# Evacuating the first PSUM transposes of a four-layer network in two pieces of two column blocks

**Chip, cores, metric.** One core of one Trainium2 chip. The metric is the device time of one execution in microseconds, here the median of several executions. The profile of a kernel is one execution; its span, from the first instruction to the last, is about 1.8 us shorter than the time of the same execution.

## The reference

Four residual layers on 2048 tokens of width 1024: linear attention, gated MLP, and the same two again, each behind a layernorm.

```python
x = A_x                                                   # 1 x 2048 x 1024, bf16
x = x + _A_ref(_layernorm(x, axis=-1), A_wqkv, A_wo)      # linear attention, 32 heads of 32
x = x + _B_ref(_layernorm(x, axis=-1), B_W_gate, B_W_up, B_W_down)   # 3584 wide, ReLU gate
x = x + _A_ref(_layernorm(x, axis=-1), A_wqkv, A_wo)
x = x + _B_ref(_layernorm(x, axis=-1), B_W_gate, B_W_up, B_W_down)
```

## The kernel before

Only the head matters here: the first 18 us, in which four row tiles of x (128 tokens each) are loaded, normalised, transposed on TensorE and multiplied with the key weights. All later transposes are made by DMA. The loads (`k0` is the first block of 512 key columns, `k1` the second, 1 MB each; ScalarE's queue where `nc.scalar` stands, else SyncE's):

```python
    for _ in range(12):                                   # warm-up of TensorE
        nc.tensor.matmul(idle, lhsT=zero[:, 0:P], rhs=zero, start=True, stop=True)
    k0, k1, v0, q0, q1 = (ring.place() for _ in range(5))
    self.load_x(0, 0)
    self.load_x(0, 1, nc.scalar)
    k0(0, H)
    self.load_x(1, None, nc.scalar)
    k0(H, 2 * H)
    self.load_x(2)
    k1()
    ...                                                   # cut: the other loads
```

Four transposes of 128x128 blocks go into one PSUM tile, and one instruction evacuates all four, that is, copies them to SBUF, where the projection matmuls read them:

```python
    def turn(j, h):
        tp = self.ps3.tile([P, H, P], BF16, tag="b")      # H = 4
        for i in range(H):
            kt = h * H + i
            nc.tensor.transpose(tp[:, i, :], xn[j][:, kt * P:(kt + 1) * P], self.ident)
        dst = self.xnT[0, 0][:, h * H:(h + 1) * H, j * P:(j + 1) * P]

        def take(engine):
            if engine == "v":
                nc.vector.tensor_copy(out=dst, in_=tp)
            else:
                nc.scalar.activation(out=dst, in_=tp, func=ACT.Copy)
        return take
```

The first unit of the head, in the order in which each engine gets its work. `k(0, 0, between)` is the projection of row tile 0 on the first key block: eight matmuls of 128x512, with `between` put in ahead of the seventh.

```python
    def block0():
        stat(0, 0); stat(0, 1); rstd(0)
        stat(1, 0)                        # statistics of row tile 1, first half
        scale(0, 0); scale(0, 1)          # normalise row tile 0 (VectorE)
        t0 = turn(0, 0)
        t1 = turn(0, 1)
        t0("s")                           # the evacuation that the change splits
        stat(1, 1); rstd(1)
        t1("v")
        k(0, 0, between)
    def between():
        scale(1, 0)
        t0 = turn(1, 0)
        scale(1, 1)
        t0("v")
```

## Time and profile before

| | before |
|---|---|
| time, median of 3 runs | 1629.09 us (1628.83 to 1629.37) |
| span of the profiled run | 1627.0 us |
| TensorE busy | 1621.9 us |
| TensorE idle for a named wait | 1.3 + 0.4 + 0.2 us, all before 7.5 us |
| first evacuation, start to first projection matmul | 6.79 to 7.44 us |

Read it from below: the kernel is a stream of matmuls with almost no gap, so a change either takes matmul time away or closes a gap; and the gaps are in the head. The lines that carry this stand in the prediction.

### The profile page before, as it was taken

To read this page: it belongs to the slowest core of one execution; us is meant where nothing else is said; L and a number is where in the kernel's file an instruction comes from. 1 tells how busy PE (TensorE), PEld (TensorE's weight loads), DVE (VectorE), ACT (ScalarE), POOL (GpSimd) and SP (SyncE) were. 2 spreads that over 40 slices of the span, in tenths; PEclk is the share of its full clock that TensorE was granted. 3 is DMA by queue.
4 is the path that set the end of the run, shared out by engine and by line. 5 is a ranking of instruction groups with operands and counts; after the bars stand their busy time and mean duration, and the time that the engine had idled before them with its cause. 6 is when DMAs were issued, how large, how long until landed. Compare 5 with 4: busy or idle time off the path is not lost.

```text
span 1627.0 us, 18776 instructions
## 1 busy us (share of the span) xinstructions
PE 1621.9 (100%) x7756; PEld 740.3 (46%) x7756; DVE 566.7 (35%) x940; ACT 331.8 (20%) x638; POOL 201.9 (12%) x134
## 2 busy tenths in 40 slices
PE   9999999999999999999999999999999999999999
PEld 4444444444444444444444444444444444444444
DVE  7845695213112212222264547932021112111211
ACT  6741212101110110111067312121011101101110
POOL 2349220000000000000023582100000000000000
PEclk9999999999999999999999999999999999999999
DMA  8313547447445445544560147464554454454452
GB/s 253 58 52 61 173 75 210 144 147 227 155 158 188 156 147 166 168 149 134 168 121 1 52 99 247 86 190 146 187 165 150 156 179 155 145 168 152 155 162 72
DMA packets 298246, 235.06 MB, mean 144 GB/s; under 512 B 101296, under 2 KB 294192, under 8 KB 298160
## 3 DMA queue, kind: packets, MB, share of 16 engines
q1 hardware_dynamic: 293120, 229.27, 48.0%
q10 hardware_dynamic: 5040, 4.59, 0.8%
q8 instruction: 60, 0.98, 0.2%
q14 instruction: 26, 0.21, 0.0%
HBM read 201.33 MB, written 8.39 MB: 129 GB/s over the span
## 4 chain that ended last, share of the span: by engine, by line
PE 98%; ACT 1%; DVE 1%; issue 0%; DMA 0%; DVEq 0%
PE pg L640 24%; PE pu L640 24%; PE acc L664 23%; PE ps L405 12%; PE ps L531 7%; PE ps L440 7%; PE kv L453 0%; PE acc_last L664 0%; ACT e L352 0%; DMA x<-in_A_x_dram 0%; ACT e L351 0%; PE fold L516 0%; DVE st L139 0%; ACT e L353 0%; DVE slab L359 0%
## 5 line engine op out<-in xcount | busy, mean ns | idle before, releaser
L640 PEld LDWEIGHTS <-t 128*128 128x128 bf16 x3584 | 350.7, 98 | 422.8
L640 PE MATMUL pg<-xnT,t 128*128 128x512 bf16 x1792 | 423.3, 379 | 0.0
L640 PE MATMUL pu<-xnT,t 128*128 128x512 bf16 x1792 | 423.3, 379 | 0.0
L664 PE MATMUL acc<-t,hT 128*128 128x512 bf16 x1764 | 382.5, 379 | 0.0
L646 DVE TENSOR_TENSOR hT<-pu,rg 128x512 bf16<-128x512 f32 x224 | 154.8, 691 | 572.1 <-PE pu L640 572.1
L645 ACT ACTIVATE rg<-pg 128x512 f32<-128x512 f32 x224 | 133.5, 596 | 737.3 <-PE pg L640 737.0
L664 PEld LDWEIGHTS <-hT 128*128 128x128 bf16 x1820 | 178.1, 98 | 209.0
L405 PE MATMUL ps<-t,xnT 128*128 128x512 bf16 x1024 | 224.1, 379 | 0.5 <-ACT xnT L268 0.4
L405 PEld LDWEIGHTS <-xnT 128*128 128x128 bf16 x1024 | 99.3, 98 | 120.2 <-issue 2.0
L531 PE MATMUL ps<-T,pqT 128*128 128x512 bf16 x512 | 111.2, 379 | 0.0
L146 ACT ACTIVATE rstd<-mv,eps 128x1 f32<-128x1 f32 x64 | 18.7, 294 | 333.8 <-DVE mv L144 333.6
L681 DVE TENSOR_TENSOR xo<-x,acc 128x512 bf16<-128x512 f32 x31 | 21.3, 688 | 170.3 <-PE acc L664 170.3
L484 POOL TENSOR_TENSOR prod<-pq,zrow 128x1024 f32<-128x1024 bf16 x32 | 68.0, 2124 | 85.9 <-DVE den L489 72.5
L139 DVE BATCH_NORM_STATS2 stats<-x 128x6 f32<-128x512 f32 (+1 forms) x120 | 78.0, 673 | 0.8
L531 PEld LDWEIGHTS <-pqT 128*128 128x128 bf16 x512 | 49.9, 98 | 60.4 <-issue 0.5
L420 POOL CAST ksum<-x 128x512 f32<-128x512 bf16 x2 | 1.7, 866 | 605.4 <-DVE x L359 605.4
L678 DVE TENSOR_TENSOR x<-x,acc 128x512 f32<-128x512 f32 x32 | 21.6, 674 | 138.5 <-PE acc L664 137.4
L422 POOL TENSOR_TENSOR ksum<-ksum,slab 128x512 f32<-128x512 f32 x46 | 54.0, 1182 | 84.6 <-DVE slab L359 75.1
L359 DVE SCALAR_TENSOR_TENSOR pq<-ps,e 128x512 bf16<-128x512 f32 x64 | 44.0, 688 | 53.9 <-ACT e L353 52.2
L496 POOL TENSOR_TENSOR pq<-pq,den 128x1024 bf16<-128x1024 bf16 x32 | 61.7, 1934 | 3.1 <-DVE den L491 3.1
L489 DVE TENSOR_REDUCE den<-prod 128x32 f32<-128x1024 f32 x32 | 38.9, 1217 | 53.9 <-POOL prod L484 53.9
L440 PE MATMUL ps<-slab,x 128*128 128x512 bf16 x256 | 56.6, 379 | 0.0
(57 smaller groups left out, 596.8 us busy)
## 6 DMA issues: line engine op xcount, KB each, us to landing
t<-in_B_W_gate_dram SPq DMA_DIRECT2D x56, 1024.0 KB, 7.0
t<-in_B_W_up_dram SPq DMA_DIRECT2D x56, 1024.0 KB, 5.4
t<-in_B_W_down_dram SPq DMA_DIRECT2D x64, 896.0 KB, 5.2
t<-in_A_wqkv_dram SPq DMA_DIRECT2D x11, 1024.0 KB, 5.1
t<-in_A_wo_dram SPq DMA_DIRECT2D x4, 1024.0 KB, 6.8
away<-x SPq DMA_DIRECT2D x8, 512.0 KB, 4.3
x<-away SPq DMA_DIRECT2D x8, 512.0 KB, 8.4
out_dram<-xo ACTq DMA_DIRECT2D x31, 128.0 KB, 2.3
```

Of the source, the lines that this page charges most:

```text
L139: self.nc.vector.bn_stats(out=stats[:, c, :], in_=src[:, c * fmax:(c + 1) * fmax])
L359: nc.vector.scalar_tensor_tensor(out=out, in0=ps, scalar=0.0, in1=e, op0=ALU.max, op1=ALU.add)
L405: nc.tensor.matmul(by_row(ps), lhsT=self.xnT[l, l_q][:, kt, j * P:(j + 1) * P], rhs=w[:, kt, :].rearrange("p (b i d) -> p i b d", i=R, d=H ...
L422: nc.gpsimd.tensor_tensor(out=ksum[:, cols], in0=ksum[:, cols], in1=pk, op=ALU.add)
L440: nc.tensor.matmul(ps, lhsT=self.xn[l, t][:, d * P:(d + 1) * P], rhs=self.pk[l, t][:, h * NW:(h + 1) * NW], start=(t == 0), stop=(t == sel ...
L484: nc.gpsimd.tensor_tensor(out=prod, in0=pq_of[sc, j], in1=zrow, op=ALU.mult)
L496: nc.gpsimd.tensor_tensor(out=heads(pq), in0=heads(pq), in1=den[:, :].unsqueeze(2).to_broadcast([P, D // HD, HD]), op=ALU.mult)
L531: nc.tensor.matmul(ps, lhsT=pqT[sc][:, g, j * P:(j + 1) * P], rhs=T[g // 2][:, g % 2, n2 * NW:(n2 + 1) * NW], start=(g == 0), stop=(g == G ...
L640: nc.tensor.matmul(ps, lhsT=w[:, kt, fi * P:(fi + 1) * P], rhs=self.xnT[l, q][:, kt, :], start=(kt == 0), stop=(kt == KT - 1))
L645: nc.scalar.activation(out=rg, in_=pg, func=ACT.Relu)
L646: nc.vector.tensor_tensor(out=h[:, fi, :], in0=pu, in1=rg, op=ALU.mult)
L664: nc.tensor.matmul(ps[:, 0:n], lhsT=hT[ft // 4][:, ft % 4, j * P:(j + 1) * P], rhs=wd[:, k, i * n:(i + 1) * n], start=(ft == 0), stop=(ft ...
```

## The change

Its intent: let the first projection matmul, which needs only the first transposed block, start when half of the evacuation is done.

```diff
             def take(engine):
                 if engine == "v":
                     nc.vector.tensor_copy(out=dst, in_=tp)
+                elif engine == "s":
+                    nc.scalar.activation(out=dst, in_=tp, func=ACT.Copy)
                 else:
-                    nc.scalar.activation(out=dst, in_=tp, func=ACT.Copy)
+                    for i in range(0, H, 2):
+                        nc.scalar.activation(out=dst[:, i:i + 2, :], in_=tp[:, i:i + 2, :],
+                                             func=ACT.Copy)
@@
-            t0("s")
+            t0("ss")
```

## The prediction

> **What bounds the kernel now.** I read the page first: busy shares, then the chain that ended last.
>
> ```profile
> PE 1621.9 (100%) x7756; PEld 740.3 (46%) x7756; DVE 566.7 (35%) x940; ACT 331.8 (20%) x638; POOL 201.9 (12%) x134
> ...
> PE 98%; ACT 1%; DVE 1%; issue 0%; DMA 0%; DVEq 0%
> ```
>
> TensorE is busy for 1621.9 of 1627.0 us and it makes 98% of the chain. So only 5.1 us of the span can be had by anything that is not fewer or faster matmuls, and ScalarE, busy 20%, is no bound in the large. The change adds and removes no matmul. It can matter only in a gap of TensorE, or where ScalarE itself is the chain. So next I asked which waits TensorE has at all, in the view of waits for that engine over the whole span (columns: us in total, times, longest):
>
> ```profile
> PE idle L221 <- DVE zero L218: 1.3, 1, 1.3
> PE ps L405 <- ACT xnT L268: 0.4, 1, 0.4
> PE tp L261 <- DVE x L155: 0.2, 1, 0.2
> ```
>
> These are three waits, all in the first 7.5 us. The middle one is the very wait that the change aims at: the first projection matmul waits for ScalarE's evacuation (L268) of the first four transposes. Then the first microseconds in order of time (start, duration, engine, line, and in brackets the idle time before):
>
> ```profile
> 5.90 0.72 DVE L155 TENSOR_SCALAR x<-x,mv,rstd 128x512 bf16<-128x512 bf16 x2
> 6.35 0.72 PE L261 MATMUL tp<-ident,x 128*128 128x128 bf16 x8 [0.21 <-DVE x L155]
> 6.79 0.60 ACT L268 ACTIVATE xnT<-tp 128x512 bf16<-128x512 bf16 x1 [1.24 <-PE tp L261]
> 7.25 0.21 DVE L144 BATCH_NORM_AGGREGATE mv<-st 128x2 f32<-128x12 f32 x1
> 7.38 0.37 DVE L266 COPY xnT<-tp 128x512 bf16<-128x512 bf16 x1
> 7.44 1.47 PE L405 MATMUL ps<-t,xnT 128*128 128x512 bf16 x6 [0.37 <-ACT xnT L268]
> 7.50 0.29 ACT L146 ACTIVATE rstd<-mv,eps 128x1 f32<-128x1 f32 x1
> 8.06 0.74 DVE L155 TENSOR_SCALAR x<-x,mv,rstd 128x512 bf16<-128x512 bf16 x2 [0.31 <-ACT rstd L147]
> 8.74 0.39 PE L261 MATMUL tp<-ident,x 128*128 128x128 bf16 x4
> 8.97 0.59 PE L405 MATMUL ps<-t,xnT 128*128 128x512 bf16 x2
> ...
> 13.31 0.60 ACT L349 ACTIVATE e<-ps 128x512 f32<-128x512 f32 x1 [0.58 <-PE ps L405]
> ...
> 13.81 1.08 ACT L268 ACTIVATE xnT<-tp 128x512 bf16<-128x512 bf16 x2
> ```
>
> The reader should see: the eight transposes end at 7.07 (6.35 + 0.72); the first evacuation starts at 6.79, as soon as its four are done, and ends at 7.39; the matmul starts 0.05 us later, at 7.44. TensorE is idle for 0.37 us in between. Then six matmuls run, at most, before four transposes of the second row tile, which need a scaling (L155) that starts at 8.06. Last, the chain of waits itself, cut to the first 10 us:
>
> ```profile
> 6.35 0.41 PE tp L261 x4
> 6.76 0.02 issue
> 6.79 0.61 ACT xnT L268
> 7.39 0.05 issue
> 7.44 1.47 PE ps L405 x6
> 8.91 0.22 PE tp L261 x4
> 9.13 0.43 PE ps L405 x2
> 9.56 0.24 PE tp L261 x4
> 9.80 0.02 issue
> 9.82 0.42 DVE xnT L266
> ```
>
> The evacuation is a link of the chain that sets the end. What is saved there is saved at the end, if nothing beside it takes over.
>
> **What the Trainium skill says.** "ScalarE: Activation LUTs", section "What ACT_TABLE_LOAD costs": an ACTIVATE with immediate scale and bias takes 186 ns + 0.833 ns per element of a partition, and back-to-back ones overlap by about 93 ns. The trace agrees roughly: 512 elements should be 612 ns, and L268 shows 597 (0.60). Two of them back to back at 13.81 take 1.08 us in place of 2 x 0.597 = 1.19, so the overlap here is 0.11. "TensorE: Matmul & The Clock Gate", section "Back-to-back issue gap": N / 2.4 + 2.5 ns for a warm matmul on its own, 216 ns for 512 columns; the six matmuls of 1.47 us with 0.379 for one give (1.47 - 0.379) / 5 = 0.218, so it agrees. "Perfetto Trace Analysis", section "DVE / Act Engine Instruction": the profile's end is when the semaphore update is pushed, and it becomes visible after that; the 0.05 us between 7.39 and 7.44 is that.
>
> **The change part by part.** The order of instructions of both builds differs in three places only: one 128x512 ACTIVATE becomes two of 128x256 on ScalarE, the ScalarE counts that later instructions wait for rise by one, and the weight load of the third projection matmul gets a wait of its own (for the second piece). TensorE, VectorE, GpSimd and the transfers have the same instructions in the same order.
>
> Removed: nothing of the start. The first piece still waits for all four transposes, since only the last of them signals. So ScalarE still starts at 6.79.
>
> First piece: 0.597 - 256 x 0.833 ns (0.213) = 0.384 us, so it ends at 6.79 + 0.384 = 7.17; the skill's formula gives 0.399. With the 0.05 the first matmul can start at 7.22 to 7.23. Are its other inputs there? Its transposes are done at 7.07 and the next four hold the TensorE no longer than that. The first half of its weights was issued at 1.19 and landed 4.5 us later, at 5.7. So the start moves from 7.44 to 7.23, a gain of 0.21.
>
> Second piece: two pieces together cost one fixed part more, less the overlap: 0.384 + 0.384 - 0.11 = 0.65 us in place of 0.60, so it ends at 6.79 + 0.65 = 7.44, visible at 7.49. The third matmul, which waits for it, would start at 7.23 + 2 x 0.217 = 7.66. There is no wait there, with 0.17 to spare.
>
> Fifth and sixth matmul: at 7.23 + 4 x 0.217 = 8.10. They need VectorE's copy (7.38 + 0.37 = 7.75) and the second half of the weights (estimate from the median of both halves, 5.2, and the first, 4.5: some 5.9 after 1.7, so 7.6). Both are in time.
>
> Beside it: ScalarE's next work, rstd (L146), starts at 7.50 because VectorE's aggregate ends at 7.46. The second piece ends at 7.44, so ScalarE's extra 0.05 us lies inside its idle time and delays nothing. The scaling of row tile 1 stays at 8.06.
>
> Next link: TensorE would now be through its six matmuls at 7.23 + 6 x 0.217 = 8.53. The first half of the scaling is one 0.41 us instruction from 8.06, done at 8.47, visible at 8.52. That is a dead heat: the transposes can start at about 8.53 in place of 8.74, but their first weight load is no longer hidden behind matmuls (98 ns for one in the groups of instructions), so between 0 and 0.1 of the 0.21 may be lost. The rest of the chain to 9.82 is TensorE alone (the other half of the scaling ends at 8.80), and from there VectorE runs without a pause to 13.15, through the statistics and the scaling of row tile 2. The x of tile 2, issued at 2.20, landed after 6.0, at 8.2, so it doesn't bind at 10.17 - 0.2.
>
> The sum: 0.21 saved, 0 to 0.1 lost again at 8.5. I take -0.18 us. 1629.09 - 0.18 = 1628.9, a hundredth of one per cent.
>
> **The rivals.** (1) Nothing arrives: a wait that is 0.2 us behind the first takes its place. The candidates are the scaling at 8.5 (above, and the nearest) and the second block of key weights: issued at 2.75, 8.4 us to landing, so there at 11.15, while its first matmul would move from 9.65 + 8 x 0.217 = 11.38 to 11.17. That is another dead heat, but TensorE has 0.1 to 0.2 us of slack before the transposes at 13.21 (they wait for VectorE's scaling), so a small wait there is hidden. If one of them takes all, the time is 1629.1. Against it: both have what is needed at the new time by the numbers, if just.
> (2) It gets slower: the second piece or its semaphore is late (the third matmul waits), or rstd is pushed back, and with it scaling, transposes and all after them. For that the pair would have to take 0.1 us more than worked out before rstd moves, and 0.22 before the third matmul moves by 0.05. Loss at most 0.1 us: 1629.2. The 0.11 overlap seen at 13.81 speaks against it.
> (3) An early start wins more than itself, by meeting a transfer or a buffer better later on. The page gives 5.1 us as the ceiling for all idle time, and the table of stretches shows TensorE busy all of 106.5 to 1600, so there is nothing to win there; a win over 0.4 would have to come from the head's 2.1 us of idle time. I hold it unlikely.
>
> **Range and chances.** The effect is 0.2 us, and three runs of the kernel before lie between 1628.83 and 1629.37, a spread of 0.54. So the range is the run-to-run spread around 1628.9 with some room for a shift by code placement or by the transfers of the head: 1628.3 to 1629.5. All three rivals are far inside 2% (32 us). Chances: faster 0.002, same 0.996, slower 0.002. I expect that the times alone will hardly tell the change from nothing and that only the trace shows it.
>
> **What would show it right or wrong.** In the profile after: two ACTIVATE of 128x256 at the evacuation's line, of 0.38 to 0.40 us each, 0.65 us together, starting at 6.8; TensorE's wait for it 0.16 in place of 0.37; the first projection matmul at 7.2; no new wait of TensorE at the third matmul; rstd still at 7.5; the second tile's transposes at 8.5 to 8.65 in place of 8.74; VectorE's copy at 9.6 to 9.75 in place of 9.82; and the sum of the span shorter by 0.1 to 0.25. Wrong would be: the first piece as long as 0.5 (a fixed cost larger than thought), a new TensorE wait for rstd's chain at 8.5 that eats it all, or a span that differs by over half a microsecond, which would mean that something outside the head moved.

## The result, and the profile after

The changed kernel took 1628.82 us (median of 6 runs, 1628.57 to 1629.45), the kernel before 1628.98 in its 6 runs (1628.76 to 1629.37). The ratio is 0.9999, interval 0.9986 to 1.0012: the same.

The median fell by 0.16, but the profiled run itself is 0.2 us longer than the one before: 1627.2. Its first microseconds in order of time, for comparison with those in the prediction:

```profile
6.44 0.76 PE L261 MATMUL tp<-ident,x 128*128 128x128 bf16 x8
...
7.02 0.66 ACT L271 ACTIVATE xnT<-tp 128x256 bf16<-128x256 bf16 x2 [1.36 <-PE tp L261]
...
7.46 1.47 PE L409 MATMUL ps<-t,xnT 128*128 128x512 bf16 x6 [0.25 <-ACT xnT L271]
...
11.93 1.89 PE L409 MATMUL ps<-t,xnT 128*128 128x512 bf16 x8 [0.37 <-DMA t<-in_A_wqkv_dram]
```

The reader should see three things. The link itself is shorter, as worked out: from the start of the evacuation to the first matmul it is 7.46 - 7.02 = 0.44 us, against 7.44 - 6.79 = 0.65 before. But the evacuation began 0.23 later, so the matmul came at the same time as before. And at 11.93 there is a wait that the profile before did not have: 0.37 us for the second key block.

The late evacuation has its cause just ahead of it. Tile 0 was scaled at 5.93 (5.90 before), so the data were as early, but TensorE was still slow: the last of the 12 warm-up matmuls took 0.63 us here and 0.38 before, and the slowest transposes and weight loads in this stretch took 314 and 152 ns (230 and 99 before). TensorE after, in order of time:

```profile
6.01 0.63 PE L221 MATMUL idle<-zero 128*128 128x512 bf16 x1
6.44 0.31 PE L261 MATMUL tp<-ident,x 128*128 128x128 bf16 x1
```

and the last warm-up matmul before:

```profile
5.77 0.38 PE L221 MATMUL idle<-zero 128*128 128x512 bf16 x1
```

I call this a low clock. The profile's granted clock (PEclk, as a share of full speed) shows 1.00 in this stretch, so here it is read from the durations; in e4 below, where matmuls of the same shape take 0.63 us again, PEclk is 0.50. "TensorE: Matmul & The Clock Gate", section "What you observe", says that the transition comes about 4 us into sustained matmul work, give or take 500 ns from run to run. The profile before agrees: its warm-up starts at 1.34 us, and the weight load at 5.16 still took 0.15 us, the one at 5.55 took 0.10, so the clock rose 3.8 to 4.2 us after the start. The profile after does not: the transpose at 6.44 was still slow, 5.1 us after the same start.

So two things that vary from run to run, each as large as the change, lay on top of it. Was the gain real and hidden, or taken back by a wait that takes the old one's place?

### The profile page after: what moved, and what is told of

It reads as the page before. It is cut to its first block, busy times and chain, and to the rows that moved or that the text cites. A ratio compares the mean times of both kernels' runs of the same rounds, so it can differ in the third digit from the quotient of the medians.

```text
span 1627.2 us, 18777 instructions
## 1 busy us (share of the span) xinstructions
PE 1622.1 (100%) x7756; PEld 740.7 (46%) x7756; DVE 566.6 (35%) x940; ACT 331.9 (20%) x639; POOL 202.1 (12%) x134
## 4 chain that ended last, share of the span: by engine, by line
PE 98%; ACT 1%; DMA 1%; issue 0%; DVE 0%; SPq 0%
PE pu L644 24%; PE pg L644 24%; PE acc L668 23%; PE ps L409 12%; PE ps L535 7%; PE ps L444 7%; DMA t<-in_A_wqkv_dram 1%; PE kv L457 0%; PE acc_last L668 0%; ACT e L356 0%; ACT e L355 0%; PE fold L520 0%; ACT e L357 0%; DVE pq L363 0%; DVE stats L139 0%
```

## The experiments

Theory A: the split moves the head, and with it the end, forward by 0.2 us, and chance hides it in some runs. Rival B: the second key block always comes too late, and the gain is always lost there. Rival C: there is nothing but noise. Runs of one call were on the same chip: the first four experiments, the next four, and the last three. To read through the noise I use landmarks of each profile (us from the span's start):

| profile | tile 0 scaled | first evacuation | first projection matmul | tile 1 transposed | tile 3 transposed | last output add |
|---|---|---|---|---|---|---|
| before | 5.90 | 6.79 | 7.44 | 8.74 | 17.37 | 1624.06 |
| after | 5.93 | 7.02 | 7.46 | 8.76 | 17.56 | 1624.25 |
| e1, changed again | 5.97 | 6.86 | 7.30 | 8.60 | 17.23 | 1623.92 |
| e11, changed, third | 5.90 | 6.79 | 7.23 | 8.54 | 17.17 | 1623.90 |
| e2, before + halves | 6.03 | 6.92 | 7.58 | 8.88 | 17.50 | 1624.19 |
| e3, changed + halves | 6.64 | 7.59 | 8.02 | 9.33 | 17.95 | 1624.64 |
| e4, five evacuations | 6.48 | 7.46 | 10.63 | 13.16 | 22.19 | 1628.88 |
| e5, two tiles | 6.15 | 6.93 | 7.37 | 8.78 | 17.41 | 1624.12 |
| e6, four pieces | 5.98 | 6.87 | 7.20 | 8.89 | 17.79 | 1624.47 |
| e7, before + halves of tile 1 | 5.62 | 6.73 | 7.38 | 9.73 | 18.36 | 1625.07 |
| e8, changed + halves of tile 1 | 5.64 | 6.53 | 6.97 | 9.35 | 17.98 | 1624.68 |

From tile 3's transposes to the last add it is 1606.68 to 1606.73 us in every row (and in e9 and e10, which the table leaves out). So in these profiles whatever a run gains or loses, it gains or loses before tile 3.

**e1: the changed kernel again, unchanged.**

> The changed kernel again, unchanged. Theory A (the split moves the head forward by 0.2 us; two things that vary from run to run, when TensorE's clock gets warm and when the second block of key weights lands, hide it in some runs): from the first evacuation to the first projection matmul 0.44 us again, not 0.65; where the weights land before 11.5 us TensorE shows no wait for them, the last tile's matmuls of the head begin at 17.65 and the span is 1626.8; where they land at 11.9 it waits 0.3 to 0.4 and the span is 1627.2. Fastest of its runs about 0.2 below the fastest of the kernel before, medians 0.1 to 0.2 apart. Rival B (the weights always come too late and the gain is always lost): a TensorE wait of 0.3 for them in this profile too, and no run under the fastest of the kernel before. Rival C (nothing but noise): fastest runs within 0.05 of each other.

Measured: 1628.62 (5 runs, 1628.53 to 1628.91) against 1629.16 for the kernel before (9 runs, 1628.75 to 1629.94), ratio 0.9997 (0.9983 to 1.001). The link is 0.44 again. The second key block landed 8.3 us after its issue at 2.75, so at 11.05, and TensorE did not wait for it. Span 1626.8. Rival B falls: here the gain came through. The fastest runs are 0.22 apart, which speaks against C.

**e2 and e3: the second key block in two halves**, in the kernel before and in the changed one, so that the first matmul needs only the first half:

```diff
-        k1()
+        k1(0, H)
+        k1(H, 2 * H)
```

> The kernel before, with the second block of key weights loaded in two halves, so that its first matmul needs only the first half. Theory A: the first half lands about 1 us earlier than the whole did, near 10.5 to 11.0 us, so no TensorE wait for it can come up; the time is that of the good runs of the kernel before, 1628.8 to 1628.9 (0 to -0.2 on the median), with less spread. Rival B, where the weights bind always: clearly faster than the kernel before, by 0.3 or more.

> The changed kernel with the same halves. Theory A: no TensorE wait for the weights, last tile's matmuls of the head at 17.6 to 17.7, median 0.15 to 0.2 us below that of the halves alone (1628.6 against 1628.8). Rival B says the same for this one, but with the gain appearing only here. Rival C: same as the halves alone within 0.05. If the scaling of row tile 1 binds at 8.5 us, only 0.1 between them.

Measured: 1628.97 (1628.84 to 1629.14) and 1628.76 (1628.42 to 1629.29), 5 runs each; ratios to the kernel before 0.9999 and 0.9998. In neither profile does TensorE wait for the key weights, and the pair lies 0.21 apart, though their ranges overlap. The landmark of 17.6 to 17.7 for e3 was missed: its profiled run is the slowest of its five, because the first load of x landed 0.8 us later than in e2 (VectorE's first statistics began at 4.25; at 3.4 to 3.6 in before, after, e1 and e2, at 4.13 in e4). The median of e2, too, missed its 1628.8 to 1628.9. The distances in the table take that out. From tile 0's scaling to the last add: e2 1618.16, e3 1618.00; kernel before 1618.16, e1 1617.95. So with the weights out of the way the split is worth 0.16 to 0.21, and the spread of the times has a third source, the landing of x.

**e4: does the end follow the first evacuation one to one?** The kernel before, with the evacuation made five times (the result is right; four copies are for nothing):

```diff
-            t0("s")
+            for _ in range(5):
+                t0("s")
```

> The kernel before, with the first evacuation made five times, one after another, on ScalarE (right result, four copies for nothing): does the end follow the first evacuation one to one? Each copy waits for the one ahead, so about 4 x 0.62 = 2.5 us on the link. Theory A: first projection matmul at about 9.9 in place of 7.4, rstd of row tile 1 2.3 later as well, end +2.3 to +2.5 us (1631.3 to 1631.5). Rival C or a head with slack in it (the end set by transfers): end +1 or less.

Measured: 1633.61 (1633.49 to 1634.06), 4.45 above the kernel before of the same rounds, not 2.5. In order of time:

```profile
10.63 2.74 PE L406 MATMUL ps<-t,xnT 128*128 128x512 bf16 x6 [2.98 <-ACT xnT L268]
...
13.16 0.63 PE L261 MATMUL tp<-ident,x 128*128 128x128 bf16 x4
```

The link itself grew as expected, from 0.65 to 10.63 - 7.46 = 3.17 us, so by 2.52. Most of the rest is the clock: after 2.98 us of idleness the six matmuls take 2.74 us in place of 1.47, and the next four transposes 0.63 in place of 0.39; PEclk is 0.50 from 10.63 to 13.37. My sum had left that out. The question is answered all the same. From the first evacuation to the transposes of tile 3 it is 22.19 - 7.46 = 14.73 us against 17.37 - 6.79 = 10.58 before, 4.15 more; to the last add it is 1621.42 against 1617.27, again 4.15 more. What the head loses, the end loses: nothing in the 1600 us between absorbs it. (The last 0.3 of the 4.45 in the medians is not taken apart.)

**e5: can the wait be cut further?** The changed kernel with the halves of e3, and the first four transposes in two PSUM tiles, so that the first piece waits for two transposes only:

```diff
-            tp = self.ps3.tile([P, H, P], BF16, tag="b")
+            own = (j, h) == (0, 0)
+            tps = [self.ps.tile([P, H // 2, P], BF16, tag="a", name=f"tpa{i}") for i in range(2)] if own else []
+            tp = None if own else self.ps3.tile([P, H, P], BF16, tag="b")
             for i in range(H):
                 kt = h * H + i
-                nc.tensor.transpose(tp[:, i, :], xn[j][:, kt * P:(kt + 1) * P], self.ident)
+                to = tps[i // 2][:, i % 2, :] if own else tp[:, i, :]
+                nc.tensor.transpose(to, xn[j][:, kt * P:(kt + 1) * P], self.ident)
@@
-                        nc.scalar.activation(out=dst[:, i:i + 2, :], in_=tp[:, i:i + 2, :],
+                        nc.scalar.activation(out=dst[:, i:i + 2, :], in_=tps[i // 2],
```

> The changed kernel with the key weights in halves, and with the first four transposes in two PSUM tiles of two, so that the first piece waits for two transposes and not for four: does a further gain at the first wait still arrive? From the first transpose to the first projection matmul 0.76 us, against 0.88 in the changed kernel's second profile and 1.09 before. But there the transposes of row tile 1 came at 8.60, just after the scaling they need (end 8.55): theory A says that this scaling binds now, first transpose to those of tile 1 stays at 2.15 to 2.2 us, TensorE shows a new wait of about 0.1 for the scaling, and the time is that of the halves with the change, 1628.6 to 1628.8. If nothing binds, another 0.12 less (2.06 and 1628.5).

Measured: 1628.73 (1628.53 to 1629.34) against 1628.94 (9 runs, 1628.69 to 1631.63), ratio 0.9997. The one run of 1631.63 weighs on all ratios of this call, which are of means; I go by the medians. In order of time:

```profile
6.61 0.40 PE L265 MATMUL tpa<-ident,x 128*128 128x128 bf16 x4 [0.26 <-DVE x L155]
...
7.37 1.47 PE L413 MATMUL ps<-t,xnT 128*128 128x512 bf16 x6
...
8.31 0.73 DVE L155 TENSOR_SCALAR x<-x,mv,rstd 128x512 bf16<-128x512 bf16 x2 [0.31 <-ACT rstd L147]
...
8.78 0.40 PE L265 MATMUL tp<-ident,x 128*128 128x128 bf16 x4
```

From the first transpose to the first matmul it is now 0.76 us, as expected, and the bracket at the matmul is gone: TensorE no longer waits for the evacuation. But the first half of tile 1's scaling ends at 8.31 + 0.41 = 8.72, and the transposes that need it follow at 8.78. From the first transpose to these it is 2.17 us (2.18 in e1, 2.39 before), and from tile 0's scaling to the last add 1617.97 (1617.95 in e1). So the further 0.12 was lost within two microseconds: the chain statistics, rstd, scaling of tile 1 binds now. The list of TensorE's waits shows no new entry for it, where I had expected one of 0.1. The weight load ahead of these transposes does show it. In e5:

```profile
8.78 0.23 PEld L265 LDWEIGHTS <-x 128*128 128x128 bf16 x4 [0.44 <-DVE x L155]
```

in e11, the changed kernel:

```profile
8.54 0.23 PEld L261 LDWEIGHTS <-x 128*128 128x128 bf16 x4 [0.33 <-DVE x L155]
```

The wait for the scaling is 0.11 longer, which is what was gained at the first matmul.

**e6: four pieces of one block**, in the changed kernel (`range(H)` and `i:i + 1` in place of `range(0, H, 2)` and `i:i + 2`).

> The changed kernel with four pieces of one block each in place of two of two. A piece of 128 elements should take about 0.28 us, so from the first evacuation to the first projection matmul 0.33 us (0.44 with two pieces, 0.65 with one), and all four end 0.77 after their start. Theory A: as in the two-tiles run the scaling of row tile 1 binds, so transposes of tile 1 are 1.74 us after the first evacuation as with two pieces, and the end no earlier than with two; later by up to 0.1 if the longer row of pieces holds up rstd.

Measured: 1628.80 (4 runs, 1628.64 to 1629.19), ratio 0.9997. A piece takes 0.28 us, the four 0.79, and the first matmul comes 7.20 - 6.87 = 0.33 after the evacuation's start, all near what was expected. The landmark at tile 1 (1.74) is not to be had from this profile: the second half of the first key block and the second block came late in it, and TensorE waited 0.23 us at the fifth matmul and 0.46 for the second block. The longer row of pieces did not hold up rstd: it started at 7.58, 0.03 after the aggregate it needs. In the median it is no better than two pieces.

**e7 and e8: tile 1 of x in halves**, before and with the split; both also with the halves of e2 and 11 warm-up matmuls. Tile 1's first statistics stand ahead of tile 0's scaling in VectorE's order and wait for the whole load of tile 1, so I expected to gain there.

```diff
-        self.load_x(1, None, nc.scalar)
+        self.load_x(1, 0, nc.scalar)
+        self.load_x(1, 1, nc.scalar)
```

> The kernel before with the row tile 1 of x loaded in two halves too (and the key weights in halves, and 11 warm-up matmuls in place of 12, so that they end before the first transposes can begin). The statistics of tile 1's first half stand in VectorE's order ahead of the scaling of tile 0, and wait for the whole load in every profile so far (to between 5.3 and 6.0 us). If that landing is what spreads the runs: VectorE waits for it no more, scaling of tile 0 at 5.6 to 5.7 in place of 5.9 to 6.6, the spread of the runs under 0.3, median 1628.6 to 1628.8 (0.3 below the kernel before). If the spread comes from somewhere else, it stays at 0.5 and over.

> The same three edits in the changed kernel: the candidate that should beat both. Theory A: 0.2 below the run without the split, 1628.4 to 1628.6, from the first evacuation to the first projection matmul 0.44 against 0.65, and first evacuation to the last output's add 1617.05 against 1617.27. Rival C: the same as without the split.

Measured: 1629.79 (1629.46 to 1629.94) and 1629.96 (1629.44 to 1630.34) against 1628.94: 0.85 and 1.02 slower in the median. (The ratios, 1.0003 and 1.0004, have intervals that include 1; the run of 1631.63 is in their mean.) Tile 0 was scaled at 5.62, as hoped. But the second half of tile 1, issued 0.48 us later, landed only after 7 us. VectorE in e7, in order of time:

```profile
7.72 0.69 DVE L139 BATCH_NORM_STATS2 st<-x 128x6 f32<-128x512 bf16 x1 [1.37 <-DMA x<-in_A_x_dram]
...
9.26 0.73 DVE L155 TENSOR_SCALAR x<-x,mv,rstd 128x512 bf16<-128x512 bf16 x2 [0.31 <-ACT rstd L147]
```

and TensorE in e8:

```profile
6.97 1.04 PE L411 MATMUL ps<-t,xnT 128*128 128x512 bf16 x4 [0.15 <-ACT xnT L273]
8.63 0.60 PE L411 MATMUL ps<-t,xnT 128*128 128x512 bf16 x2 [0.62 <-DVE xnT L268]
```

The pair is a useful control. The split does its local work in e8 as well (0.44, against 0.65 in e7), and then TensorE stands at the fifth matmul, since VectorE's copy of the other four transposes comes after the statistics that wait for x. With the chain led through the landing of tile 1, the split is worth nothing: from that landing's statistics (7.72 and 7.35) to the last add it is 1617.35 in e7 and 1617.33 in e8.

**e9 and e10: tile 1 of x ahead of the key weights**, before and with the split, to repair that pair (the halves of e2 and the 11 warm-up matmuls, also in these two, are cut from the diff):

```diff
         self.load_x(0, 1, nc.scalar)
+        self.load_x(1, 0)
+        self.load_x(1, 1, nc.scalar)
         k0(0, H)
-        self.load_x(1, None, nc.scalar)
-        k0(H, 2 * H)
+        k0(H, 2 * H, nc.scalar)
```

> The kernel before with the loads at the head in another order: row tile 1 of x in two halves, one on each of the two queues, ahead of the first key weights (the last pair of runs had it behind them, and its second half landed at 7.3 to 7.7 us and cost 0.8), second half of the first key weights on ScalarE's queue, second key weights in halves, 11 warm-up matmuls. If the place in the queues is what made that pair slow: both halves of tile 1 are there by 5.0 and 6.2, tile 0 is scaled at 5.6, VectorE shows no wait for x after 4 us, scaling of tile 1 at 7.8, and the time is 0.3 below the kernel before, 1628.6 to 1628.8. If a half of any load simply takes longer, 1629 or more.

> The same loads with the split: candidate to beat both kernels. Theory A: first evacuation at 6.5, first projection matmul 0.44 later against 0.65 without the split, and 0.2 us below that run, 1628.4 to 1628.6. If a transfer (second half of the first key weights, some 6.9 to 8.0 us) holds up the fifth matmul, the split is worth less than 0.1, as it was in the last pair.

Measured: 1631.65 (1629.65 to 1633.28) and 1631.66 (1630.41 to 1633.64) against 1628.88: 2.8 slower, ratios 1.0014 and 1.0017. Tile 1 came early, as planned, but now the first key weights are late. The list of TensorE's waits in e9:

```profile
PE ps L407 <- DMA t<-in_A_wqkv_dram: 2.8, 1, 2.8
```

Their first half, issued at 1.66 us in place of 1.19, landed 8.3 us after issue in place of 4.5 (8.1 in e10). Again the clock fell after the wait (six matmuls in 2.36 us, PEclk 0.50 from 10.45 on). The order of loads in the kernel before was the better one, and no candidate of mine beats the changed kernel. Why this load took four microseconds longer is open. Its later issue alone doesn't account for it: in the kernel before, the second half, equally large and issued at the same 1.66, took 5.8. In e9 and e10 the second half was also issued at 1.67 on the other queue, and no run parts the two. And both profiles are of slow runs (1633.07 and 1633.64, against fastest runs of 1629.65 and 1630.41), so the delay is not the same in every run.

**e11: the changed kernel a third time.**

> The changed kernel a third time, for the times: over all runs so far the changed kernel's median was 1628.66 (11 runs) and that of the kernel before 1629.09 (15 runs of the first two chips). Theory A: median 0.1 to 0.3 below the runs of the kernel before on this chip, its fastest run about 0.2 below their fastest; from first evacuation to first projection matmul 0.44. Rival C: no difference beyond 0.05 in either.

Measured: 1628.86 (5 runs, 1628.57 to 1628.94) against 1628.88 (9 runs, 1628.77 to 1629.24), ratio 1.0 (0.9987 to 1.0012). In the medians of this call there is next to nothing, so the 0.1 to 0.3 that I expected there was missed; the fastest runs are 0.20 apart. Its profile happens to match the one before in everything that varies: tile 0 scaled at 5.90, the clock warm in the warm-up's last matmul, evacuation at 6.79, second key block at 2.75 + 8.2 = 10.95. In order of time:

```profile
6.79 0.66 ACT L271 ACTIVATE xnT<-tp 128x256 bf16<-128x256 bf16 x2 [1.11 <-PE tp L261]
7.50 0.30 ACT L146 ACTIVATE rstd<-mv,eps 128x1 f32<-128x1 f32 x1
```

TensorE alone, in order of time:

```profile
6.36 0.72 PE L261 MATMUL tp<-ident,x 128*128 128x128 bf16 x8
7.23 1.47 PE L409 MATMUL ps<-t,xnT 128*128 128x512 bf16 x6 [0.15 <-ACT xnT L271]
8.54 0.40 PE L261 MATMUL tp<-ident,x 128*128 128x128 bf16 x4
...
17.17 0.62 PE L261 MATMUL tp<-ident,x 128*128 128x128 bf16 x8
```

And the chain of waits at its end, in the kernel before:

```profile
1624.06 0.42 DVE xo L681
```

in e11:

```profile
1623.90 0.42 DVE xo L685
```

Laid beside the lines of before in the prediction, this is the change with the landmarks ahead of it unmoved: same evacuation start, matmul 0.21 earlier, tile 1 0.20, tile 3 0.20, last add 0.16.

All runs together: the kernel before had 33, median 1628.94, the fastest 1628.69; the changed one 16, median 1628.66, the fastest 1628.53. Nine of the 16 are below every one of the 33. This pools chips and calls; call by call the medians are 0.16, 0.54 and 0.02 apart, so it is the matched profiles and not the medians that give the gain its size.

## Why the prediction was right

The time was right: 1628.82 for 1628.9, well within the range. By itself that says little, since no change at all (1628.98) lies in that range too, and that 0.16 came so near to 0.18 is luck, with medians that differ by 0.02 to 0.54 from call to call. The mechanism was right, though the first profile could not show it. Of the signs that the prediction named, the profile after has the pieces (0.38 each, 0.66 together) and no wait at the third matmul; it misses the start of the evacuation (7.02 for 6.8), TensorE's wait (0.25 for 0.16), the first matmul (7.46 for 7.2), tile 1's transposes (8.76 for 8.5 to 8.65), VectorE's copy (9.84 for 9.6 to 9.75) and the span (0.2 longer for 0.1 to 0.25 shorter). e11, where the landings and the clock match the profile before, has them:

- First piece 0.384 us: measured 0.38. Pair 0.65: 0.66. First matmul at 7.23: 7.23 in e11, and 0.43 to 0.44 us after the evacuation's start in every profile with two pieces (e10 apart, whose weights came late). TensorE's wait 0.16: 0.15 in e1 and e11.
- No wait at the third matmul, rstd not pushed back: rstd at 7.50 in e11, and no TensorE wait between the first matmul and the sixth.
- The dead heat at 8.5 us, with 0 to 0.1 of the gain lost: nothing was lost in e1 and e11 (tile 1 1.74 to 1.75 us after the evacuation, 1.95 before). But the heat was as close as it looked: e5 gained another 0.12 at the first wait and got none of it past this point.
- The gain arrives at the end: 0.16 to 0.21 by landmarks; e4 showed 4.15 for 4.15. VectorE's copy: 9.63 in e11. Span: 1626.8, so 0.2 shorter.

The weak step was the rival about the second key block. I took 11.15 us from one trace as its landing, called it a second dead heat, and held a late arrival to be hidden by 0.1 to 0.2 us of slack. In the six profiles with this load undivided it landed at 10.95, 11.05, 11.15, 11.55, 11.89 and 12.12. In the two latest (after and e6) TensorE waited 0.37 and 0.46, and in the first of them, the profile of the result, this and the cold clock took back more than the split gave. The slack itself was sized rightly: from tile 1's transposes to tile 3's it is 8.63 us in before, e1 and e11, 8.80 in after and 8.90 in e6, so of the two waits 0.17 and 0.27 arrived and 0.2 was hidden. What was wrong was the landing. The second half of the first key block has the same flaw: the prediction took 7.6 for it, the six profiles have it at 7.3 to 8.4, and in e6 the fifth matmul waited for it. A landing time has a spread, and both steps should have used one. The range covered it only because I had taken the spread of the runs for its width, without knowing what makes it. The clock of TensorE in the warm-up was not in the prediction at all.

## What to carry to other kernels

Where TensorE is busy all the time, as it is here, the head is where a small wait still counts in full, and splitting an evacuation so that the consumer starts on the first piece is worth the difference of the two durations, until the next chain, here the normalisation of the second tile, is reached; more pieces give nothing then. An effect of 0.01% can't be read from a median of a few runs, nor from one profile: take distances between landmarks inside each profile, find what varies ahead of them (landing of a load, clock), and compare profiles in which those agree. And leave the order of the first loads alone unless it is measured: in the reordering of e9 the first weights, issued half a microsecond later, landed 8.3 us after issue in place of 4.5.

## What the Trainium skill lacked or had wrong

- "TensorE: Matmul & The Clock Gate", section "What's actually happening", gives at least one idle window of about 3.4 us before the clock falls. Here gaps of 2.98 us (e4) and 2.75 us (e9) were enough: the six matmuls after them took 2.74 and 2.36 us, against 1.47, with PEclk at 0.50 (in e9 only from 0.45 us after the gap had ended).
- The same page, section "What you observe": its 500 ns either way were exceeded in the profile after, where the transpose at 6.44 was still slow 5.1 us after the start of the warm-up.
- "ScalarE: Activation LUTs", section "What ACT_TABLE_LOAD costs": its 186 ns + 0.833 ns per element is 2 to 5% too high for copies from PSUM here (292 ns for 128 elements, 0.28 measured; 399 for 256, 0.38; 612 for 512, 0.597), and the overlap of neighbours was 0.10 to 0.11 us for pairs, not 0.093.
- None of the pages I used gives the spread of a landing time: the same 1 MB load, issued at 2.75 us each time, took 8.2 to 9.4 us in six profiles, and a 512 KB load issued 0.47 us later, behind two small ones and beside its other half, took 8.3 us in place of 4.5.
